# Single unread matmuls between the first products of a layer on TensorE

## The chip, the core and the metric

The kernel runs on one core of one Trainium2 chip. The core has TensorE (PE in the profile: matrix products, with PEld for the loads of its weights), VectorE (DVE), ScalarE (ACT), GpSimd (POOL) and SyncE (SP), which issues most DMAs. Each engine works through its own instructions in order and waits on semaphores for the others. The metric is the device time of one execution in microseconds, the median of several runs; lower is better.

## What is computed

An attention with two kinds of window is followed by two layers of a perceptron. All inputs and the output are float32.

```python
scores = q @ k.T / sqrt(D)            # B, H, S, D = 4, 8, 576, 64
# heads 0-3: each query sees the 32 keys up to itself
# heads 4-7: each fourth key of the 128 up to itself
attn = softmax(where(mask, scores, -1e9))
x = attn @ v                          # to 2304 tokens x 512
h = x @ w_in;  g = maximum(0.01 * h, h);                 x = g @ w_out     # 512 -> 2048 -> 512
h = x @ w_in2; g = maximum(h, 0) + log1p(exp(-abs(h)));  out = g @ w_out2
```

## The kernel before

**Stages.** Tokens are worked through in blocks. Attention runs by pairs of heads and windows of 288 tokens: transposes of q and k on PE (`pe_trans`, line 536), scores (`scores_early`, lines 585 and 589), maxima over partitions on GpSimd (line 640), the difference on VectorE (line 644), the exponential on ScalarE (line 647), the product with v (`pv`, line 665), the reciprocal and the scaling on VectorE (lines 675 to 677), a transpose back (`xT`, line 686) and a split of x into a high and a low half (lines 743 and 747).

The first layer needs a product of x with `w_in` (`g1`, "first-product", twelve matmuls of line 769) and one of the activated result with `w_out` (`g2`, "second-product", line 812), for each of 16 slices of the 2048 hidden columns. The float32 operands are split into a high and a low half, so each product takes three matmuls where one would do. The weights of the first layer come from memory as float32, are converted on ScalarE and VectorE (lines 304 to 322) and split (lines 361 and 364: the low half of a slice is the last to be ready). The second layer follows the first one.

**What sets the order.** All work is written as a list of `Op`s, each with an engine, a cost in the planner's microseconds, its dependencies and the buffers it takes and gives back. `run_schedule` goes through them in a simulated time and writes out each engine's instructions in the order that it finds. Nothing is reordered on the chip.

**Spins.** `spin(n)` (line 436) issues n matmuls that nobody reads: 288 columns of bf16 constants, into a PSUM tile in buffer y3. The list has 150 Ops of three such matmuls (`NSPIN`), each booked at 0.37 us. They are `optional`: their priority is last, and from the first first-product on (`opened`, lines 230 to 233) they are dropped without cost. Before that the planner takes one where PE has nothing ready, or, from 8 us on (`FILL`, line 208), before an operation that has just become ready. 14 such groups, 42 matmuls, are in the program.

A spin's tile is taken from a pool with one buffer for y3. A new tile in it waits until what was done with the old one is over; within one tile the three matmuls do not wait for each other. The buffer holds a bank of the attention before (a score bank, copied out by ScalarE at line 603), and of the second-product's sums from its first use on (`yp3`, line 805).

Of the kernel before, what the change touches and what calls it, by code (L numbers as in the profile page):

```python
# [26 lines left out]
def kernel(  # L27
# [80 lines left out]
    def run_schedule(slots):  # L108

        late = {"dma": 2.0, "pe": LATPE}  # L110
        lib = ["reduce"]

        def switch(o):
            return SWITCH if o.lib and o.lib != lib[0] else 0.0

        for o in ops:
            for d in o.deps:
                d.users.append(o)
            for d in o.order:
                d.next.append(o)  # L120

        def lag(a, b):
            if b.eng == "bw":
                return 2.0
            return late.get(a.eng, LATS if a.eng == b.eng else LAT) + b.slack

        left = {o: len(o.deps) + len(o.order) for o in ops}
        order = [o for o in ops if not left[o]]
        for o in order:
            for u in o.users + o.next:  # L130
                left[u] -= 1
                if not left[u]:
                    order.append(u)
        assert len(order) == len(ops)
        for o in reversed(order):
            t = [1e9 if o.target is None else o.target]
            t += [u.raw - o.cost - lag(o, u) for u in o.users]
            t += [u.raw - o.cost for u in o.next]
            o.raw = min(t)
            if o.lead is not None:  # L140
                o.earliest = max(o.earliest, o.raw - o.lead)
            o.prio = 1e6 if o.optional else o.raw - o.margin
        free = dict(slots)
        ready_at = {}
        left = {o: len(o.deps) + len(o.order) for o in ops}
        engines = sorted({o.eng for o in ops})
        pools = {e: [] for e in engines}
        busy = {e: BUSY.get(e, 0.0) for e in engines}
        events = [0.0] + list(BUSY.values())
        for o in ops:  # L150
            if not left[o]:
                ready_at[o] = o.earliest
                heapq.heappush(events, o.earliest)
                pools[o.eng].append(o)

        def done(u, t):
            left[u] -= 1
            ready_at[u] = max(ready_at.get(u, u.earliest), t)
            if not left[u]:
                pools[u.eng].append(u)  # L160
                heapq.heappush(events, ready_at[u])

        coming = {e: [] for e in engines}
        unbegun = {o: len(o.deps) + len(o.order) for o in ops}
        due = {o: o.earliest for o in ops}

        def begins(u, t):
            unbegun[u] -= 1
            due[u] = max(due[u], t)
            if not unbegun[u]:  # L170
                coming[u.eng].append(u)

        result = []
        now = locked = 0.0
        opened = False
        filled = []
        finish, held = [], []
        while True:
            moved = False
            while held and held[0][0] <= now + 1e-9:  # L180
                for r in heapq.heappop(held)[2].rel:
                    free[r] += 1
            while finish and finish[0][0] <= now + 1e-9:
                _, _, o = heapq.heappop(finish)
                if o.hold:
                    heapq.heappush(held, (o.end + o.hold, o.n, o))
                    heapq.heappush(events, o.end + o.hold)
                else:
                    for r in o.rel:
                        free[r] += 1  # L190
                for u in o.users:
                    done(u, o.end + lag(o, u))
            for e in engines:
                if busy[e] > now + 1e-9 or not pools[e]:
                    continue
                best = None
                for o in pools[e]:
                    if ready_at[o] <= now + 1e-9 and all(free[a] >= o.acq.count(a) for a in o.acq):
                        rank = o.prio + (HOLD if switch(o) else 0.0) + (WAIT if o.lock and now < locked else 0.0), o.n
                        if best is None or rank < best_rank:  # L200
                            best, best_rank = o, rank
                if best is None:
                    continue
                if e == "pe" and not opened and not best.optional and now - ready_at[best] < 0.3:

                    for o in pools[e]:
                        if o.optional and ready_at[o] <= now + 1e-9 and all(free[a] >= o.acq.count(a) for a in o.acq):
                            if result[-1:] != [o] and now > FILL and not (filled and filled[-1] is best):
                                filled.append(best)
                                best = o  # L210
                            break
                if e in ("dve", "act") and now > AHEAD_FROM:

                    soon = [u for u in coming[e] if now + 1e-9 < due[u] <= now + min(AHEAD, best.cost)
                            and u.prio < best.prio - GAP and all(free[a] >= u.acq.count(a) for a in u.acq)]
                    if soon:
                        heapq.heappush(events, min(due[u] for u in soon))
                        continue
                pools[e].remove(best)
                if best in coming[e]:  # L220
                    coming[e].remove(best)
                for a in best.acq:
                    free[a] -= 1
                best.start, best.end = now, now + best.cost + switch(best)

                if best.lib == "reduce":
                    locked = now + LOCK
                if best.lock and now < locked:
                    best.end = locked + best.cost
                if best.fn is g1:  # L230
                    opened = True
                if best.optional and opened:
                    best.end, best.skip = now, True
                if best.lib:
                    lib[0] = best.lib
                busy[e] = best.end
                heapq.heappush(finish, (best.end, best.n, best))
                heapq.heappush(events, best.end)
                for u in best.users:
                    begins(u, best.end + lag(best, u))  # L240
                for u in best.next:
                    begins(u, best.end if u.eng == e else now)
                    done(u, best.end if u.eng == e else now)
                result.append(best)
                moved = True
            if len(result) == len(ops):
                break
            if moved:
                continue
            while events and events[0] <= now + 1e-9:  # L250
                heapq.heappop(events)
            assert events, "the schedule is stuck"
            now = events[0]
        return result
# [502 lines left out]
    order = [(0, f) for f in range(LEAD)]  # L757
# [289 lines left out]
    LAG = 2  # L1047
    NCOPY = 2
    FILL = 8.0
    NSPIN, LOCK, SLACK0, SLACK, HOLDS = 150, 1.2, 0.3, 1.0, 1.5  # L1050
    SLACKT = 2.0
    AHEAD_FROM, AHEAD, GAP = 480.0, 0.9, 2.0
# [30 lines left out]
    spins = []  # L1083
    for i in range(NSPIN):
        spins.append(Op("pe", 0.37, spin, 3, order=spins[-1:], acq=["y3"], rel=["y3"], start=3.2, target=1e6, optional=True))
    y_free = {3: spins}
    reduces = []
    last_att, last_conv = [], []
    pairs, xready = [], {}
# [8 lines left out]
    for w in range(NW):  # L1098
# [3 lines left out]
        for p in range(NPAIR):  # L1102
# [14 lines left out]
            if early:  # L1117
                if p % 2 == 0:
                    ls = []
                    for which in (1, 0):  # L1120
                        qd = "dma" if which or w else "act"
                        nb = 4 if dil or w and which else 3
                        o = Op(qd, 0.48 * nb, a.load_rows, which, nc.scalar if qd == "act" else nc.sync,
                               acq=[f"rows{which}" if dil else "raw"],
                               order=[o for o in row_loads if o.earlier < w], **m)
# [5 lines left out]
            else:  # L1131
# [3 lines left out]
                           order=[] if early else [a.lq, prev(1, "lv")], **m)  # L1135
# [3 lines left out]
            if early:  # L1139
                banks = [f"y{2 * (p % 2) + which}" for which in range(2)]  # L1140
                rel = [["rows0" if dil else "raw"], ["rows1" if dil else "raw"]] if p % 2 else [[], []]
# [15 lines left out]
            if early:  # L1157
                tags = a.banks()[1]
                sc = a.o_s1 = Op("pe", 1.35 if dil else 1.15, a.scores_early, deps=[tk] + tq,
                                 order=[prev(1, "o_s1")], acq=tags + [tag_s], **ms)  # L1160
# [5 lines left out]
            else:  # L1166
                blk = 0.29 if dil else 0.33
                s0 = Op("pe", 2 * blk, a.scores, 0, deps=[tk] + tq, acq=["at", tag_s],
                        order=[prev(1, "o_s1")], **ms)
# [4 lines left out]
                   target=TR + p * 2.1 if w == 1 else None, **m)  # L1174
# [5 lines left out]
            if turned:  # L1180
                pv = a.o_pv = Op("pe", 0.9, a.pv_late, deps=x + [lv],
                                 order=[prev(1, "o_pv")], acq=["at", "xn"], **ms)
# [5 lines left out]
            for half in range(2 if dil else 1) if not turned else ():  # L1188
                pv = Op("pe", 0.58 if dil else 0.85, a.pv, half, deps=x + [lv],
                        order=pvs[-1:] or [prev(1, "o_pv")],  # L1190
# [319 lines left out]
```

## Time and profile before

| | us |
|---|---|
| three runs | 910.30, 910.72, 911.47 |
| median | 910.72 |
| profiled execution | 913.61 |
| its span, from the first to the last instruction | 911.5 |

PE is busy for 881.6 us of the span, DVE for 655.4, ACT for 393.7, POOL for 137.1. A matmul row of the profile counts as busy from its start to its modelled end, and successive matmuls overlap, so the step from one start to the next tells what a matmul costs in a stream. The granted clock of TensorE is either 2.4 GHz (1.00) or 1.2 GHz (0.50).

### The profile page before, as it was taken

The numbers are of one execution on the slowest core, as the hardware profiler recorded it, in microseconds if no ns is written. First come the engines' busy times: TensorE is split into PE (matmuls) and PEld (weight loads), VectorE is DVE, ScalarE is ACT, GpSimd is POOL, SyncE is SP. The second block draws the span as 40 slices with busy tenths as digits, with TensorE's granted clock in tenths as the row PEclk, the third lists the DMA queues.
The fourth block names the chain that finished last, engine by engine and source line by source line (L and its number), as shares of the span: only waits on it lengthen the run. The fifth ranks groups of instructions, "written<-read, shape, count | busy, mean of one in ns | idle before, by whom it ended". The sixth has DMA issues, their size and how long they took to land.

```text
span 911.5 us, 16342 instructions
## 1 busy us (share of the span) xinstructions
PE 881.6 (97%) x6376; PEld 825.5 (91%) x6376; DVE 655.4 (72%) x1189; ACT 393.7 (43%) x763; POOL 137.1 (15%) x73
## 2 busy tenths in 40 slices
PE   6889999999999999999999999999999999999998
PEld 4779999999989989998999999989888988888886
DVE  3989995476797897996975586765765775576563
ACT  2767763343344444444445563323422432243222
POOL 4500020010252351442420000000000000000000
PEclk9979999999999999999999999999999999999999
DMA  8879122255545455454237877632453353235332
GB/s 228 224 212 307 21 36 50 75 121 169 164 112 157 113 148 172 131 145 165 88 117 262 278 251 222 194 93 93 139 156 101 115 172 105 93 116 144 111 93 93
DMA packets 157985, 131.89 MB, mean 145 GB/s; under 512 B 102100, under 2 KB 138964, under 8 KB 157908
## 3 DMA queue, kind: packets, MB, share of 16 engines
q1 hardware_dynamic: 155508, 130.26, 48.3%
q8 instruction: 50, 0.82, 0.4%
q10 hardware_dynamic: 2400, 0.59, 0.3%
q14 instruction: 27, 0.22, 0.1%
HBM read 104.60 MB, written 26.21 MB: 144 GB/s over the span
## 4 chain that ended last, share of the span: by engine, by line
PE 51%; DVE 2%; POOL 0%; issue 0%; ACT 0%; POOLq 0%
PE yo L1018 22%; PE h L945 17%; PE yp L812 5%; PE h L769 4%; PE hp L1006 2%; DVE cf L322 0%; DVE cf L313 0%; POOL mx L640 0%; PE sc L616 0%; DVE xn L712 0%; DVE gl L794 0%; DVE cs L332 0%; PE pv L696 0%; DVE rd L717 0%; DVE s L644 0%
## 5 line engine op out<-in xcount | busy, mean ns | idle before, releaser
L812 PE MATMUL yp<-gh,w 128*128 128x288 f32 (+2 forms) x1024 | 230.1, 299 | 4.1 <-DVE ys L822 2.0
L769 PE MATMUL h<-xh,w 128*128 128x288 f32 (+2 forms) x1024 | 231.2, 301 | 1.1 <-DVE w L364 1.1
L1018 PE MATMUL yo<-wo,w 128*128 128x512 f32 x864 | 222.9, 395 | 0.0
L945 PEld LDWEIGHTS h<-tr,w 128*128 128x128 f32 x1344 | 174.4, 188 | 11.1
L812 PEld LDWEIGHTS yp<-gh,w 128*128 128x128 f32 x1024 | 171.8, 188 | 6.3 <-DVE ys L822 3.5
L1018 PEld LDWEIGHTS yo<-wo,w 128*128 128x128 f32 x864 | 152.5, 188 | 27.1
L945 PE MATMUL h<-tr,w 128*128 128x256 f32 x1344 | 176.8, 279 | 0.0
L769 PEld LDWEIGHTS h<-xh,w 128*128 128x128 f32 x1024 | 173.0, 190 | 2.4 <-DVE w L364 1.6
L769 PE MATMUL h<-xl,w 128*128 128x288 f32 (+2 forms) x512 | 152.2, 297 | 0.7 <-DVE xl L747 0.7
L812 PE MATMUL yp<-gl,w 128*128 128x288 f32 (+2 forms) x512 | 151.0, 295 | 0.3 <-DVE gl L794 0.3
L983 ACT ACTIVATE ex<-ex 128x512 f32<-128x512 f32 x72 | 45.5, 632 | 152.2 <-DVE ex L980 151.9
L785 ACT ACTIVATE hc<-h 128x288 f32<-128x288 f32 (+2 forms) x128 | 51.8, 404 | 109.9 <-PE h L769 108.7
L769 PEld LDWEIGHTS h<-xl,w 128*128 128x128 f32 x512 | 97.2, 190 | 1.2 <-DVE xl L747 1.2
L812 PEld LDWEIGHTS yp<-gl,w 128*128 128x128 f32 x512 | 96.2, 188 | 0.6 <-DVE gl L794 0.5
L794 DVE TENSOR_TENSOR gl<-hc,gh 128x288 fp32r<-128x288 f32 (+2 forms) x128 | 65.3, 512 | 36.1 <-ACT gh L790 35.4
L640 POOL PARTITION_ALL_REDUCE mx<-s x24 | 50.0, 2084 | 268.3 <-DVE s L630 244.2
L986 DVE SCALAR_TENSOR_TENSOR ex<-hs,ex 128x512 f32<-128x512 f32 x64 | 44.3, 692 | 32.8 <-ACT ex L983 32.3
L704 POOL PARTITION_ALL_REDUCE sm<-s x16 | 61.6, 3850 | 39.2 <-ACT s L647 39.2
L304 ACT ACTIVATE cf<-raw 128x512 f32<-128x512 f32 (+1 forms) x48 | 39.9, 831 | 57.0 <-DMA raw<-in_moe_w_in_dram 30.0
L991 ACT ACTIVATE w<-ex 128x512 fp32r<-128x512 f32 x72 | 45.3, 629 | 34.1 <-DVE ex L986 34.1
L995 DVE TENSOR_TENSOR w<-ex,w 128x512 fp32r<-128x512 f32 x72 | 49.7, 691 | 11.7 <-ACT w L991 6.8
L790 ACT ACTIVATE gh<-hc 128x288 fp32r<-128x288 f32 (+2 forms) x128 | 56.7, 443 | 3.0
(103 smaller groups left out, 980.8 us busy)
## 6 DMA issues: line engine op xcount, KB each, us to landing
wo<-w2o SPq DMA_DIRECT2D x80, 512.0 KB
raw<-in_moe_w_in_dram SPq DMA_DIRECT2D x32, 512.0 KB
raw<-in_moe_w_out_dram SPq DMA_DIRECT2D x32, 512.0 KB
w2o<-cf SPq DMA_DIRECT2D x16, 512.0 KB
out_dram<-o SPq DMA_DIRECT2D x36, 128.0 KB
w2a<-cf SPq DMA_DIRECT2D x8, 512.0 KB
w2s<-cs SPq DMA_DIRECT2D x8, 512.0 KB
w<-w2a SPq DMA_DIRECT2D x8, 512.0 KB
```

The source lines that it names most:

```text
L640: nc.gpsimd.partition_all_reduce(self.mx, self.sf, channels=P, reduce_op=bass_isa.ReduceOp.max)
L704: nc.gpsimd.partition_all_reduce(self.sm, self.sf, channels=P, reduce_op=bass_isa.ReduceOp.add)
L769: nc.tensor.matmul(out=h, lhsT=a[:, c, :], rhs=b_[:, c, :], start=(c == 0 and a is whi and b_ is xh), stop=(c == NC - 1 and a is wlo))
L785: nc.scalar.activation(out=hc, in_=hbank.pop(s), func=AF.Prelu, alpha=0.01)
L790: nc.scalar.activation(out=gh, in_=hcopy[s], func=AF.Copy)
L794: eng.tensor_sub(out=gl, in0=hcopy.pop(s), in1=gparts[s][0].bitcast(F32))
L812: nc.tensor.matmul(out=ybank[e][:, o:o + n], lhsT=a[:, e * P:(e + 1) * P], rhs=b_, start=(f == 0 and n == unit_len[u] and a is whi and b_ ...
L945: nc.tensor.matmul(out=bank[m, b][:, half], lhsT=w[:, a, kb * P:(kb + 1) * P], rhs=t[:, b_, kb], start=(kb == 0 and a + b_ == 0), stop=(kb ...
L983: nc.scalar.activation(out=self.ex, in_=self.ex, func=AF.Softplus)
L991: nc.scalar.activation(out=self.gh, in_=self.ex, func=AF.Copy)
L995: nc.vector.tensor_sub(out=self.gl, in0=self.ex, in1=self.gh.bitcast(F32))
L1018: nc.tensor.matmul(out=obank[c, t], lhsT=a, rhs=b_, start=(opens and n == 0), stop=(closes and n == 2))
```

## The change

51 single spins are put into PE's instructions between the first first-product and the first second-product. A second list of 160 optional Ops, `fills`, stands behind the old list: `spin(1)`, one matmul and one tile each, booked at 0.125 us. They are dropped only from the first second-product on (`closed`), and are passed over while an operation of PE becomes due within the next 0.2 us of the planner's time. The groups of three are dropped from the first first-product on as before.

```diff
-        opened = False
+        opened = begun = closed = False
...
+                        if o.optional and o.args[0] == 1 and begun and not closed and any(
+                                u is not o and not u.optional and now < due[u] < now + 0.2 for u in coming["pe"]):
+                            continue
...
-                if best.fn is g1:
-                    opened = True
-                if best.optional and opened:
+                begun = begun or best.fn is g1
+                closed = closed or best.fn is g2
+                opened = begun
+                if best.optional and (closed if best.args[0] == 1 else begun):
                     best.end, best.skip = now, True
...
+    NFILL = 160
...
-    y_free = {3: spins}
+    fills = []
+    for i in range(NFILL):
+        fills.append(Op("pe", 0.125, spin, 1, order=(fills or spins)[-1:], acq=["y3"], rel=["y3"], target=1e6, optional=True))
+    y_free = {3: spins + fills}
```

The instructions of VectorE, ScalarE, GpSimd and SyncE stand in the order of before. On PE the 51 spins, each with a load of its weights, stand in five trains: 5 behind the first first-product, 17 behind the transposes that follow it, 14 behind the next P·V (sixteen matmuls in the profile, eight here), 3 behind the second first-product, 12 behind the next transposes. The old instructions of PE keep their order among themselves. The line numbers of the changed kernel are higher by 4 in the functions shown here (spin 443, transpose 690, P·V 669, first-product 773).

PE before, from the end of the first first-product (`h_644`) over the transposes (`xt`) and P·V (`pv`) to the second first-product (`h_717`); what stands in brackets is the engines or DMA queues that the instruction waits for:

```order
L769 MATMUL h_644<-xh_489,w_496 128x256
L686 MATMUL xt_678<-ident_85,xn_625 128x96 [waits DVE_49,PE_49]
L686 MATMUL xt_678<-ident_85,xn_625 128x96 x2
L665 MATMUL pv_697<-lent_102 72x65 [waits DMAHW5_49,PE_49,Activation_49]
L665 MATMUL pv_697<-lent_102 72x65 [waits DMAHW6_49]
L665 MATMUL pv_697<-lent_102 72x65 x2
L665 MATMUL pv_703<-lent_102 72x65 [waits DVE_49,PE_49]
L665 MATMUL pv_703<-lent_102 72x65 x3
L769 MATMUL h_717<-xh_489,w_672 128x256
```

PE in the changed kernel, around the same transposes (now `xt_688`), with the last spins of the first train and the first of the second:

```order
L443 MATMUL spin_682<-masksb_88,identb_87 128x288 [waits PE_49]
L443 LDWEIGHTS identb_87
L443 MATMUL spin_684<-masksb_88,identb_87 128x288 [waits PE_49]
L690 MATMUL xt_688<-ident_85,xn_625 128x96 [waits DVE_49]
L690 MATMUL xt_688<-ident_85,xn_625 128x96 x2
L443 LDWEIGHTS identb_87
L443 MATMUL spin_699<-masksb_88,identb_87 128x288 [waits PE_49]
L443 LDWEIGHTS identb_87
L443 MATMUL spin_701<-masksb_88,identb_87 128x288 [waits PE_49]
```

Each spin is a tile of its own (another number) with a wait for PE; the first of all waits for ScalarE instead.

PE in the changed kernel, from the end of the second train over the same P·V (now `pv_741`, `pv_747`) to the third train:

```order
L443 MATMUL spin_736<-masksb_88,identb_87 128x288 [waits PE_49]
L669 MATMUL pv_741<-lent_102 72x65 [waits DMAHW5_49,Activation_49]
L669 MATMUL pv_741<-lent_102 72x65 [waits DMAHW6_49]
L669 MATMUL pv_741<-lent_102 72x65 x2
L669 MATMUL pv_747<-lent_102 72x65 [waits DVE_49]
L669 MATMUL pv_747<-lent_102 72x65 x3
L443 LDWEIGHTS identb_87
L443 MATMUL spin_752<-masksb_88,identb_87 128x288 [waits PE_49]
```

P·V stands behind 17 spins and ahead of 14 where it stood between the transposes and the second first-product.

## Rows read from the trace of the kernel before

**Rows 1.** The page's first part: busy us, share of the span, instructions.
```profile
PE 881.6 (97%) x6376; PEld 825.5 (91%) x6376; DVE 655.4 (72%) x1189; ACT 393.7 (43%) x763; POOL 137.1 (15%) x73
```

**Rows 2.** Table by stage: length, busy us (instructions) by engine, granted clock, DMA share, GB/s.
```profile
0.00:15.80 15.80, 6.97 (x28) 4.03 (x29) 6.03 (x4) 1.54 (x2) 7.39 (x23) 1.00 0.92 257
15.80:44.80 29.00, 25.76 (x300) 21.46 (x298) 22.97 (x39) 22.46 (x49) 15.59 (x9) 1.00 0.79 210
44.80:49.90 5.10, 3.35 (x36) 3.06 (x34) 5.03 (x12) 3.32 (x9) 2.47 (x1) 1.00 0.40 76
49.90:60.15 10.25, 8.15 (x46) 7.63 (x45) 7.86 (x18) 7.90 (x12) 0.00 (x0) 0.50 0.69 176
60.15:911.50 851.35, 837.35 (x5977) 789.37 (x5975) 613.47 (x1119) 358.53 (x693) 111.62 (x40) 1.00 0.47 140
...
60.00:130.00 70.00, 70.00 (x601) 69.81 (x600) 67.66 (x100) 52.26 (x83) 6.69 (x3) 1.00 0.50 154
```

**Rows 3.** PE in order of time: start us, us, instruction, [idle before, releaser].
```profile
46.16 0.28 PE L769 MATMUL h<-xh,w 128*128 128x256 f32 x1
46.27 0.41 PE L686 MATMUL xt<-ident,xn 96*128 96x96 f32 x3
48.29 1.58 PE L665 MATMUL pv<-lent 104*72 104x65 f32 x16 [1.60 <-ACT lent L647]
49.67 0.36 PE L769 MATMUL h<-xh,w 128*128 128x256 f32 x1
...
51.34 0.80 PE L769 MATMUL h<-xh,w 128*128 128x256 f32 x2 [1.09 <-DVE w L364]
...
53.64 0.68 PE L686 MATMUL xt<-ident,xn 72*128 72x72 f32 x4
55.34 1.23 PE L665 MATMUL pv<-lent 104*72 104x65 f32 x8 [1.01 <-ACT lent L647]
56.32 0.56 PE L769 MATMUL h<-xh,w 128*128 128x256 f32 x1
...
59.03 1.15 PE L665 MATMUL pv<-lent 104*72 104x65 f32 x8
59.97 0.47 PE L808 MATMUL yp<-zero,identb 128*128 128x512 bf16 x1
...
62.63 0.28 PE L769 MATMUL h<-xh,w 128*128 128x256 f32 x1
...
64.03 0.28 PE L812 MATMUL yp<-gh,w 128*128 128x256 f32 x1
```

**Rows 4.** Spins by stretch: duration ns min/median/max, first and last start us.
```profile
L439 PE MATMUL spin<-masksb,identb x21: 397/444/448, 8.5 to 14.5; 128*128 128x288 bf16 x21
...
L439 PE MATMUL spin<-masksb,identb x21: 283/284/296, 16.5 to 41.9; 128*128 128x288 bf16 x21
```

**Rows 5.** PE in order of time, in small windows at two groups of spins.
```profile
8.91 0.45 PE L439 MATMUL spin<-masksb,identb 128*128 128x288 bf16 x1
9.42 0.40 PE L439 MATMUL spin<-masksb,identb 128*128 128x288 bf16 x1
...
41.41 0.42 PE L686 MATMUL xt<-ident,xn 72*128 72x72 f32 x4
41.66 0.53 PE L439 MATMUL spin<-masksb,identb 128*128 128x288 bf16 x3
41.91 0.28 PE L439 MATMUL spin<-masksb,identb 128*128 128x288 bf16 x1
42.03 0.28 PE L585 MATMUL sc<-masksb,identb 128*128 128x288 bf16 x1
42.25 0.28 PE L585 MATMUL sc<-masksb,identb 128*128 128x288 bf16 x1
```

**Rows 6.** Who waited for whom, 44.7 to 64 us, DVE: us in total, times, longest.
```profile
DVE rd L675 <- PE pv L665: 2.1, 2, 1.7
```

**Rows 7.** The same for PE from 60 us to the end.
```profile
PE sc L616 <- DVE xn L724: 2.3, 2, 1.6
...
PE yp L812 <- DVE gl L794: 0.3, 1, 0.3
```

## The prediction, made before the run

> **What bounds the kernel now.** I read the busy table of the page first: TensorE (PE) is busy 97% of the span, VectorE (DVE) 72%, the others less [rows 1]. Then the table by stage, for where the missing 3% lies and at which clock PE works [rows 2]. From 60.15 us to the end PE is busy 837.35 of 851.35 us at granted clock 1.00, and from 60 to 130 us without any gap. So past 60 us the end is set by PE, and what shifts the first second-product (line 812, at 59.97) shifts nearly everything behind it. Ahead of that lies the stretch that the change touches: 44.8 to 49.9 with PE busy 3.35 of 5.10 us at clock 1.00, and 49.9 to 60.15 with PE busy 8.15 of 10.25 us at clock 0.50, that is 1.2 instead of 2.4 GHz.
>
> Third comes the order of PE's work in that stretch [rows 3]. Three idle times are to be seen: 1.60 us ahead of the product P·V at 48.29 (for the exponential on ScalarE), 1.09 ahead of the third matmul of the second first-product at 51.34 (for the low half of its weights on DVE), and 1.01 ahead of P·V at 55.34 (exponential again). And the same work costs more at the lower level: the twelve matmuls of a first-product take 2.71 us (56.32 to 59.03) and 1.40 us at the full one (62.63 to 64.03); eight matmuls of P·V take 0.94 us (59.03 to 59.97) against half of 1.38 (sixteen, 48.29 to 49.67), 0.69. So of what could be had here, the 3.70 us of idle time are not in a fill's reach, since other engines end them; the slow clock is.
>
> **What the change adds.** By the order of instructions nothing moves on DVE, ScalarE, GpSimd or the DMA queues. PE gets 51 matmuls of 288 columns ("spins", line 439), each with a weight load: 5 after the first first-product, 17 after the transpose behind it, 14 after the P·V that follows, 3 after the second first-product, 12 after the transposes behind that. The planner books 0.125 us for each. That is the pace of spins that don't wait for each other: three take from 41.66 to 42.03, 0.12 us each [rows 5].
>
> But these don't run so. A spin of the old kind is one tile of three matmuls; a new one is a tile of its own in the same PSUM buffer y3, and so each carries a wait for PE itself: it starts when the one before it has ended (all but the first of the 51 have that wait). What such a wait costs can be read off twice in the trace of before [rows 5]. At the full clock: the third spin of a group starts at 41.91 and takes 0.28; the second score matmul (line 585), which goes into the same buffer and waits for that spin, starts at 42.25. That is 0.34 us from start to start instead of 0.12. At the lower level, where spins take 444 ns at the median and not 284 [rows 4]: a group's last spin starts at 8.91 and takes 0.45, and the next group, which waits for it, starts at 9.42, so 0.06 us after its end. A spin that starts a group takes 0.40 there, so a single one costs 0.40 + 0.06 = 0.46 us, and at most 0.51 (8.91 to 9.42). The last spin of a train costs only its streaming, 0.12 or 0.24 us, where what follows doesn't wait for it.
>
> **The sum with the clock full throughout.** A train of n spins takes (n-1) x 0.34 + 0.12: 1.48, 5.56, 4.54, 0.80 and 3.86 us. PE's path, from the end of the first first-product at 46.27 [rows 3]: train of 5 to 47.75; transposes 0.25 (as 41.41 to 41.66, [rows 5]) to 48.00; train of 17 to 53.56; sixteen P·V 1.38 to 54.94; train of 14 to 59.48; first-product 1.40 to 60.88; train of 3 to 61.68; transposes 0.25 to 61.93; train of 12 to 65.79; P·V 0.69 to 66.48; first-product 1.40 to 67.88; P·V 0.69 to 68.57. Before, the second-product was reached at 59.97: 8.6 us later. The three idle times of before are inside this (what ended them, at 48.29, 51.34 and 55.34, is long there), and so is the gain from the clock. Nothing else is late: the engines that fed PE here run as before until they come to something that PE delays, DVE at the reciprocal of P·V (line 675), which already stood for PE twice, 2.1 us in all [rows 6]. DVE takes its work in order, so it stands there and doesn't run ahead. The delay thus passes to it whole.
>
> **The clock.** Whether the spins hold it is the open cost. In before it fell at 49.9, in a stretch with PE partly idle, and came back at 60.15, after PE had worked without a gap from 55.34 [rows 2, 3]. A self-waiting spin streams for 0.12 of its 0.34 us. And the trace shows a stretch of spins with self-waits that did not bring the clock up: 21 of them from 8.5 to 14.5 us, the fastest 397 ns, all at the lower level, with one wait in three spins rather than in each [rows 4]. (The stage table writes 1.00 for 0 to 15.8; the durations say otherwise.) So I take it that trains of 17, 14 and 12 such spins don't hold the full clock, and that it falls at about 49.9 as before. How long it stays down has two ends: not at all, 8.6 us in sum; or until the second-product. For the latter: of the train of 17, six steps at 0.34 and ten at 0.46, to 48.00 + 2.04 + 4.60 + 0.24 = 54.88; P·V 1.88 to 56.76; train of 14, 13 x 0.46 + 0.24 = 6.22, to 62.98; first-product 2.71 to 65.69, which is 4.8 us behind the sum above; then train of 3 +0.4, transposes +0.25, train of 12 +1.4, P·V +0.25, first-product +1.3, P·V +0.25, in all 3.9 more: 8.6 + 4.8 + 3.9 = 17.3 us. Between them I take the clock low from 49.9 to the end of that first-product, the first work without waits that PE meets, and full behind it: 8.6 + 4.8 = 13.4 us. This is nearest to the row of before, where gapless work brought it back.
>
> A rule bears on this. The Trainium skill (TensorE: Matmul & The Clock Gate, "Why this matters for your kernels") puts drops of the clock in mid-kernel down to longer idle gaps between bursts of matmuls. By it these spins, 0.06 us apart, hold the clock, and the sum is the 8.6 us of the first rival. The trace doesn't quite agree: here the clock fell with no gap of PE longer than 1.60 us.
>
> **From the profile to the time.** The profiled execution took 913.61 us with a span of 911.5, 2.1 us outside it, and lies 2.9 us over the median of the three runs, 910.72. With 13.4 us more it would be 927.0 with a span of 924.9. On the median: 910.72 + 13.4 = 924.1 us.
>
> **Rivals.**
> - *The spins hold the clock.* For it: a spin is in flight for 0.28 of each 0.34 us, and PE never stands idle for longer than 0.06. Against it: the 21 spins at the start. Time: 910.72 + 8.6 = 919.3 us.
> - *The self-waits cost nothing, and the fills do what the planner booked.* Then the trains take 0.61, 2.07, 1.71, 0.37 and 1.46 us, and the same path gives: transposes at 46.88, P·V at 49.20, first-product at 52.29, transposes at 54.06, P·V at 55.77, first-product at 56.46, second-product at 57.86 + 0.69 = 58.55, 1.4 us earlier than before: 909.3 us, faster than before. For it: the work at the lower level is there to be won, and the weights and exponentials are ready by then. Against it: 41.91 to 42.25. There are 46 steps from spin to spin, so it turns into a loss from a step of 0.12 + 1.4/46 = 0.15 us on; the row shows 0.34.
> - *The delay is given back behind 60 us.* PE waits there six times over for DVE and ScalarE, from 2.3 us for scores to 0.3 for a low half [rows 7], 9.4 us in all six rows. If those engines were ahead by then, that could be saved: 924.1 - 9.4 = 914.7 us. Against it: they stand in order behind work that PE delays, above all DVE at line 675, and DVE is busy 67.66 of the 70 us from 60 to 130 [rows 2], so it can't get ahead.
>
> **How the numbers follow.** Clock lost for part of the stretch (924.1): 0.55. Clock held (919.3): 0.32. Fills without cost (909.3): 0.07. Given back (914.7): 0.06. A measurement of this kernel can tell about 0.2% (1.8 us) from no change. The third case, at -0.15%, lies inside this bound by its sum and outside it with a little more, so I split it: faster 0.03, same 0.04, slower 0.93. The range leaves out the last two cases, 0.13. Its low end is the held clock less some tenths, 918.5; its high end the clock low to the second-product, 910.72 + 17.3 = 928.0, with half of what steps of 0.51 in place of 0.46 would add (36 such steps, 1.8 us): 929.
>
> **What would show it.** In the profile after, spins at 46.3 to about 70 us that start 0.34 us apart at the full clock and about 0.46 at the lower one; no idle time ahead of P·V and the first-products, since PE comes there last; DVE idle for several us ahead of line 675; the first second-product at 68 to 77 us instead of 59.97; from there on the same picture as before, shifted. If the clock reads 1.00 through the stretch, the first rival holds; if the spins start 0.12 us apart, the second; if the second-product is late by more than the end of the span, the third. The forecast is wrong altogether if a spin's wait for its predecessor is free.

## The result and the profile after

The changed kernel takes 920.92 us (median of four runs, 919.92 to 922.90) against 910.53 for the kernel before: 1.0115 of its time, 95% interval 1.0096 to 1.0133, 10.4 us more. The forecast was 924.1 us in a range of 918.5 to 929.0. This kernel's time moves by some us from execution to execution and between chips (on the three chips of the experiments the kernel before had medians of 913.16, 912.92 and 910.90, with single runs from 909.3 to 920.4), so the experiments are compared by their ratio to the kernel before on the same chip, and by stages of their traces.

The table by stage of the changed kernel (length, busy us and instructions of PE, PEld, DVE, ACT, POOL, granted clock, DMA share, GB/s) answers to [rows 2]. 45.45 is the end of the first first-product (46.27 before), 71.55 about the start of the first second-product (59.97 before):

```profile
45.45:51.26 5.81, 4.92 (x23) 1.92 (x22) 5.10 (x7) 3.63 (x8) 1.25 (x1) 1.00 0.51 92
51.26:64.90 13.64, 12.58 (x50) 6.85 (x50) 4.25 (x10) 2.35 (x5) 0.00 (x0) 0.50 0.85 248
64.90:71.55 6.65, 6.04 (x45) 3.91 (x45) 2.21 (x6) 3.33 (x7) 0.00 (x0) 1.00 1.02 372
71.55:917.80 846.25, 836.57 (x5978) 789.45 (x5977) 614.89 (x1120) 359.82 (x695) 111.81 (x40) 1.00 0.45 136
```

The clock still falls, 51.26 instead of 49.9, and is down longer: 13.64 us instead of 10.25. PE's order of time in the stretch answers to [rows 3]:

```profile
45.33 0.27 PE L773 MATMUL h<-xh,w 128*128 128x256 f32 x1
45.45 1.65 PE L443 MATMUL spin<-masksb,identb 128*128 128x288 bf16 x5
46.94 0.41 PE L690 MATMUL xt<-ident,xn 96*128 96x96 f32 x3
47.18 6.27 PE L443 MATMUL spin<-masksb,identb 128*128 128x288 bf16 x17
53.25 2.11 PE L669 MATMUL pv<-lent 104*72 104x65 f32 x16
55.16 6.34 PE L443 MATMUL spin<-masksb,identb 128*128 128x288 bf16 x14
61.12 0.59 PE L773 MATMUL h<-xh,w 128*128 128x256 f32 x1
...
63.86 1.28 PE L443 MATMUL spin<-masksb,identb 128*128 128x288 bf16 x3
64.97 0.42 PE L690 MATMUL xt<-ident,xn 72*128 72x72 f32 x4
65.23 4.01 PE L443 MATMUL spin<-masksb,identb 128*128 128x288 bf16 x12
69.08 0.68 PE L669 MATMUL pv<-lent 104*72 104x65 f32 x8
69.57 0.37 PE L773 MATMUL h<-xh,w 128*128 128x256 f32 x1
...
71.06 0.68 PE L669 MATMUL pv<-lent 104*72 104x65 f32 x8
71.60 0.47 PE L816 MATMUL yp<-gh,w 128*128 128x256 f32 x1
```

No row carries an idle time any more, where three did: PE has become the last to come everywhere. It counts as busy on the profile's page, 893.4 us against 881.6, but much of a spin's row is its wait: 5 of them take 1.49 us from 45.45 to 46.94, 4 x 0.34 + 0.12. VectorE and ScalarE wait now (44.7 to 75 us; before, VectorE 2.1 us for P·V [rows 6] and 0.2 for `xh`, ScalarE 2.4 for `h`):

```profile
DVE rd L679 <- PE pv L669: 7.1, 2, 3.8
DVE xl L751 <- ACT xh L747: 7.0, 1, 7.0
ACT hc L789 <- PE h L773: 14.6, 2, 11.3
```

VectorE's 7.0 us for `xh` (58.9 to 65.9) come by way of ScalarE, which stood 11.3 us (52.8 to 64.1) for the second first-product and splits x only behind it.

### The profile page after: what moved, and what is told of

It is laid out like the page before. It is cut to its first block, busy times and chain, and to the rows that moved or that the text cites. A ratio compares the mean times of both kernels' runs of the same rounds, so it can differ in the third digit from the quotient of the medians.

```text
span 917.8 us, 16439 instructions
## 1 busy us (share of the span) xinstructions
PE 893.4 (97%) x6426; PEld 828.4 (90%) x6427; DVE 656.9 (72%) x1189; ACT 394.4 (43%) x763; POOL 137.3 (15%) x73
## 4 chain that ended last, share of the span: by engine, by line
PE 50%; DVE 2%; POOL 0%; issue 0%; ACT 0%; POOLq 0%
PE yo L1022 22%; PE h L949 17%; PE yp L816 4%; PE h L773 4%; PE hp L1010 2%; DVE cf L326 0%; DVE cf L317 0%; POOL mx L644 0%; DVE gl L798 0%; DVE xn L716 0%; DVE cs L336 0%; PE sc L620 0%; DVE s L648 0%; PE pv L700 0%; DVE qz L575 0%
## 5 line engine op out<-in xcount | busy, mean ns | idle before, releaser
L949 PEld LDWEIGHTS h<-tr,w 128*128 128x128 f32 x1344 | 174.3, 188 | 11.1
L1022 PEld LDWEIGHTS yo<-wo,w 128*128 128x128 f32 x864 | 152.5, 188 | 27.1
L999 DVE TENSOR_TENSOR w<-ex,w 128x512 fp32r<-128x512 f32 x72 | 49.8, 691 | 11.7 <-ACT w L995 6.8
```

What stands on the lines that cost most here:

```text
L949: nc.tensor.matmul(out=bank[m, b][:, half], lhsT=w[:, a, kb * P:(kb + 1) * P], rhs=t[:, b_, kb], start=(kb == 0 and a + b_ == 0), stop=(kb ...
L999: nc.vector.tensor_sub(out=self.gl, in0=self.ex, in1=self.gh.bitcast(F32))
L1022: nc.tensor.matmul(out=obank[c, t], lhsT=a, rhs=b_, start=(opens and n == 0), stop=(closes and n == 2))
```

## Experiments

### The kernel before, and the changed one, a second time

The kernels are unchanged: e1 is the kernel before, e5 the changed one.

> The kernel before once more, for a second trace. The forecast was 13.4 us more; on PE's path up to the first second-product the two traces differ by 12.4 us (13.70 from the end of the first first-product before, 26.1 after), but the spans differ by only 6.3 us and the medians by 10.4. Theory 1: the first trace of before was a long execution (2.9 us over the median), with more waiting of PE behind 60 us (9.4 us in all) than is usual; then this one has about 6 to 7 us of such waits and a span near 908.6. Theory 2: the waits behind 60 us are always 9 to 10 us in this kernel, and the changed kernel gives some 4 us of its delay back there; then they are 9 to 10 us again here and the span is 908 to 909 for another reason.

> The changed kernel once more, beside e8 on one chip. Its first trace had the second-product 12.4 us later by PE's path and a span only 6.3 us (against the first trace of before) or 9.4 us (against the second, e1) longer. Theory 1 (what came back behind 60 us was chance: VectorE stood for a DMA of the second layer's weights for 1.0 us there, 4.5 to 8.2 in three of the other traces): this time the waits of PE behind 60 us are 7 to 9 us again, and the time is 920 to 924. Theory 2 (a late second-product always gets some 4 us back): 5 us of waits again, 919 to 921.

e1 took 910.5 us in its single run, 2.7 us under the median of the kernel before on its chip, with a span of 908.4. PE's waits behind 60 us add up to 8.6 us (9.4 in the first trace), which lies between the two theories of e1 and nearer to theory 2. Whether the changed kernel gives something back there is left to e5. In e1 the clock was down for a shorter time than in the first trace, 6.82 us:

```profile
45.40:51.20 5.80, 2.87 (x29) 2.37 (x28) 5.73 (x11) 3.72 (x8) 1.26 (x1) 1.00 0.47 85
51.20:58.02 6.82, 5.71 (x35) 5.50 (x33) 5.68 (x13) 5.27 (x10) 0.00 (x0) 0.50 0.84 222
```

e5 took 924.03 us (922.11 to 926.50), 1.0127 of the kernel before, interval 1.0105 to 1.0150. Its second-product starts at 73.72, 27.8 us behind the end of the first first-product at 45.88, since the clock fell twice, from 52.40 to 66.05 and again from 69.47 to 72.88. PE's waits behind 60 us are 8.4 us, where the first trace of the changed kernel had 5.3, and nothing of the delay is given back in its span, 923.7:

```profile
52.40:66.05 13.65, 12.69 (x53) 7.38 (x53) 4.24 (x10) 2.33 (x5) 0.00 (x0) 0.50 0.90 278
69.47:72.88 3.41, 3.35 (x20) 3.17 (x19) 1.79 (x4) 0.00 (x0) 0.00 (x0) 0.50 0.53 194
```

So theory 1 of e5 is borne out, its time at the very top of what theory 1 gave: what came back behind 60 us in the first trace does not come back whenever the second-product is late. From the second-product to the end of the span it is 851.5 us in the first trace of before, 850.0 in e1, 850.0 in e5, and 850.3 and 851.5 in e3 and e8 below, which are also late. The first trace of the changed kernel has 846.2, the least of all; the other traces, none of them so late, have 847.7 to 852.6. Why that one execution was shorter stays open. VectorE's wait for the store of a converted weight piece (line 313, `w2s`, 75 to 480 us) was 1.0 us in it, 4.9 in the first trace of before and 3.4 in e5, but PE's waits don't follow it: e3 has 8.2 us of it and 7.2 us of waits of PE.

### All spins in one tile: without the wait

```diff
+    filler = {}
+
+    def fill(n):
+        if "ps" not in filler:
+            filler["ps"] = ps_y.tile([P, NI * QP], F32, tag="y3", name="spin")
+        for i in range(n):
+            nc.tensor.matmul(
+                out=filler["ps"], lhsT=ident_b, rhs=masks_b.rearrange("p i m -> p (i m)"), start=True, stop=True)
...
-                o.fn(*o.args)
+                if o.fn is spin and o.args[0] == 1:
+                    fill(1)
+                else:
+                    o.fn(*o.args)
```

> The changed kernel with all 51 single spins in one tile, so that none waits for the one before it; number and places are the same. Theory (the wait for the predecessor is the cost): spins start 0.12 us apart, the trains take 0.61, 2.07, 1.71, 0.37 and 1.46 us, the clock stays at 1.00, the second-product is reached 1.4 us earlier than in the kernel before, and the time is 909.1 us (908.3 to 910.3). Rival (it is the 51 matmuls as such, or where they stand): 915 us or more.

Measured 909.0 us (906.43 to 910.32), 0.9941 of the kernel before, interval 0.9921 to 0.9961. The same 51 matmuls at the same places, and only the first one waits. PE in order of time, and then the stage table:

```profile
46.17 0.79 PE L452 MATMUL spin<-masksb,identb 128*128 128x288 bf16 x5
46.79 0.41 PE L699 MATMUL xt<-ident,xn 96*128 96x96 f32 x3
47.04 2.25 PE L452 MATMUL spin<-masksb,identb 128*128 128x288 bf16 x17
49.13 1.20 PE L678 MATMUL pv<-lent 104*72 104x65 f32 x16
```

```profile
45.00:58.00 13.00, 13.00 (x127) 11.76 (x126) 12.48 (x27) 10.60 (x20) 2.43 (x1) 1.00 0.64 154
```

17 spins now take 2.09 us (47.04 to 49.13) instead of 6.07, the clock stays at 1.00 from 45 to 58 us, and the second-product starts near 57.9, 11.7 us behind the first first-product: 2.0 us less than in the first trace of before, 1.2 less than in e1 (45.4 to about 58.3, 12.9), and 14.4 less than in the changed kernel. So the wait is the cost, and spins at the pace that the planner books are a gain of 0.4 to 0.8%.

### Two buffers in turn: half the wait

```diff
...
+            tag = ("y3", "y2")[filler[0] % 2]
+            filler[0] += 1
+            ps = ps_y.tile([P, NI * QP], F32, tag=tag, name="spin")
...
```

> The 51 single spins as in the changed kernel, each a tile of its own, but in two PSUM buffers in turn (y3 and y2), so that each waits for the last but one. Theory (the wait sets the step): the step is half of 0.34, 0.17 us, the trains take 0.80, 2.84, 2.33, 0.46 and 1.99 us, the clock holds or falls for a short time, and PE's path from the first first-product to the second-product is 14.5 us (13.7 before, 26.1 in the changed kernel): 911.3 us (910 to 914). Rival (each tile of its own costs its 0.34 us whatever it waits for): 920.9.

Measured 911.3 us (908.73 to 917.93), 0.9988 of the kernel before, interval 0.9967 to 1.0009. This is as expected, and not told apart from the kernel before. PE in order of time, and then the stage table:

```profile
45.24 0.98 PE L453 MATMUL spin<-masksb,identb 128*128 128x288 bf16 x5
46.06 0.41 PE L700 MATMUL xt<-ident,xn 96*128 96x96 f32 x3
46.31 3.00 PE L453 MATMUL spin<-masksb,identb 128*128 128x288 bf16 x17
49.15 1.20 PE L679 MATMUL pv<-lent 104*72 104x65 f32 x16
```

```profile
45.20:59.00 13.80, 13.80 (x116) 10.25 (x116) 11.31 (x23) 9.36 (x17) 1.30 (x1) 1.00 0.62 147
```

17 spins take 2.84 us (46.31 to 49.15), 16 x 0.17 + 0.12, to the hundredth what half the step gives. The stretch is 13.8 us long with the clock kept, as long as with the idle times and the slow clock in the first trace of before (13.7). The rival is out: each spin still has a tile of its own, but with twice the distance to the last one in its buffer the step is half as long.

### Trains as long, without waits: the clock's part

```diff
+        trains, inside = [12, 46, 37, 7, 32], False
         for o in schedule:
...
+            if o.fn is spin and o.args[0] == 1:
+                if not inside:
+                    fill(trains.pop(0))
+                    inside = True
+                continue
...
```

Here `fill` is that of e2, so all spins are in one tile.

> As e2, but with trains of 12, 46, 37, 7 and 32 spins in one tile: each train is as long as the changed kernel's would be at the full clock (1.48, 5.56, 4.54, 0.80, 3.86 us), without self-waits. Theory (the self-waiting spins lost the clock, and that cost 3 to 4 us on top of their length): clock 1.00 throughout, second-product 8.6 us later than in the kernel before, time some 3 to 4 us under the changed kernel's, 917 to 919. Rival (the length of the trains is all, the clock costs nothing): the changed kernel's 920.9. Second rival (part of any delay is given back behind 60 us): 914 to 916.

> e3 once more, beside e5 on one chip, to price the clock: both have trains of the same length at the full clock, but only the changed kernel's wait for themselves. Theory (the clock lost 4.2 us on PE's path, 26.1 against 21.9): 3 to 4 us faster than e5. Rival (the length of the trains is all): the same as e5.

e3 took 919.84 us (918.33 to 920.60), 1.0064 (1.0042 to 1.0086), a little over the 917 to 919 expected; e8 921.21 (919.24 to 926.53), 1.0104 (1.0077 to 1.0131). The times alone, 0.6 and 1.0% over the kernel before, would leave room for the rival in which some of the delay is given back; the traces don't, with 850.3 and 851.5 us from the second-product to the end. The stage from the end of the first first-product to the second-product, e3 and then e8:

```profile
45.50:67.50 22.00, 22.00 (x200) 18.72 (x200) 11.60 (x23) 9.47 (x17) 1.31 (x1) 1.00 0.78 233
```

```profile
45.20:67.10 21.90, 21.90 (x200) 18.66 (x199) 11.49 (x23) 9.36 (x17) 1.24 (x1) 1.00 0.78 214
```

Both keep the clock at 1.00 through 134 spins without waits, and take 21.9 us over the stretch. That is 8.2 us more than before, near the 8.6 that the sum gives for the clock held, and 4.2 us less than the changed kernel's 26.1, or 5.9 less than the 27.8 of e5. In the traces, then, the clock costs the changed kernel 4 to 6 us. By the times it is less clear: e8 is 2.8 us faster than e5 on the same chip (3 to 4 expected), but the intervals of the two ratios overlap. The rival without a cost of the clock is out by the stage tables; by the times alone it is not.

### Trains that fit the idle times

The loop is that of e3, first with the trains of e4 and e9, all in one tile:

```diff
...
+        trains, inside = [0, 12, 9, 0, 8], False
...
```

and then with those of e7 and e10, where `fill` calls `spin(1)`, so that each has its wait:

```diff
+    def fill(n):
+        for i in range(n):
+            spin(1)
...
+        trains, inside = [0, 5, 4, 0, 3], False
...
```

> As e2, but with trains of 0, 12, 9, 0 and 8 spins, so that each about fills the idle time of the kernel before and doesn't outlast it. Theory: P-V starts at 48.3 as before, the second first-product at 51.1 and ends a microsecond earlier at the full clock, the exponential behind it comes earlier, and the second-product is reached 2.5 to 3 us earlier: 907.8 us (907 to 909). Rival (the clock falls with these few spins too, or the gain is given back to VectorE behind 60 us): 910.5, no change.

> As e4, idle times filled and not outlasted, but with self-waiting single spins at 0.34 us a step: trains of 0, 5, 4, 0 and 3 instead of 0, 12, 9, 0 and 8. Theory (self-waiting spins don't hold the clock): it falls at about 50 us as in the kernel before, nothing is won, 910.5 us. Rival (any spin in flight holds it; the changed kernel only had too many): the time of e4, 907.4, with clock 1.00.

e4 took 907.4 us (906.22 to 909.09), 0.9928 (0.9903 to 0.9953); e7 910.41 (908.02 to 917.15), 0.9985 (0.9965 to 1.0005). e4 gained more against its chip's 913.16 than was expected (0.7% for 0.3%). By the times the theory of e7 seemed right, by the trace it wasn't. The stretch to the second-product, e4 and then e7:

```profile
45.20:56.40 11.20, 10.09 (x95) 8.51 (x94) 10.99 (x23) 9.10 (x17) 1.30 (x1) 1.00 0.60 154
```

```profile
46.10:57.30 11.20, 9.48 (x78) 6.85 (x78) 10.99 (x23) 9.09 (x17) 1.31 (x1) 1.00 0.68 167
```

Both take 11.2 us at clock 1.00: with twelve self-waiting spins in short trains the clock stayed up as with 29 dense ones. In e7's trace the clock had fallen earlier, at 32 us, ahead of all fills, and come back at 39. So both ran once more on one chip.

> e4 once more, beside e10 on one chip. In their traces PE's path from the first first-product to the second-product is the same, 11.1 us (e4: 45.25 to about 56.3; e7: 46.16 to 57.27), against 13.7 in the kernel before, and the clock is 1.00 through it in both; yet e4 took 907.4 us on one chip and e7 910.4 on another. Theory 1 (the difference is the chip, or clock falls ahead of the stretch, as at 32 us in e7's trace, which have nothing to do with the self-wait): the same time as e10, both 2 to 3 us under the kernel before. Theory 2 (self-waiting spins lose the clock in most executions, only not in the one that was traced): e10 is 2 to 3 us slower than this one.

> e7 once more, beside e9 on one chip: theory 1 the same time as e9, 907 to 908.5; theory 2 2 to 3 us more than e9, about the kernel before.

e9 took 906.73 us (906.27 to 907.73), 0.9961 (0.9946 to 0.9976); e10 908.77 (906.93 to 913.38), 0.9980 (0.9967 to 0.9993). Neither theory holds as it stood. e10 is 2.0 us behind e9, as theory 2 has it, but the two intervals overlap, and its trace shows again a fall ahead of the fills, as theory 1 has it, which held until they began:

```profile
33.13:53.61 20.48, 20.21 (x131) 18.35 (x131) 14.60 (x33) 11.70 (x23) 5.89 (x3) 0.50 0.77 203
53.61:63.50 9.89, 8.49 (x74) 6.33 (x73) 9.27 (x21) 8.60 (x16) 0.00 (x0) 1.00 0.79 226
```

From 53.61 on, with the self-waiting spins, the clock is 1.00. Of e10's twelve runs the three with a mean granted clock of 0.999 or 1.000 took 906.9 to 908.5 us, the others, at 0.988 to 0.997, 907.4 to 913.4. Whether those lost the clock before the fills, as the traced one, or within them, the runs don't tell, since there is one trace of each label. e4 and e9 are the fastest kernels here, 0.4 to 0.7% under the kernel before.

## Why the prediction was right, point by point

**The wait is the cost: right.** The step that decided, that a single spin waits for the one before it and so costs 0.34 us and not the 0.125 of the planner, holds to the hundredth: 1.49 us for five against 1.48 forecast, 3.85 for twelve against 3.86. e2 shows it by taking the wait away, e6 by halving it. The rival in which waits cost nothing is what e2 shows once the wait is gone: its second-product comes 1.2 to 2.0 us earlier than before, where the rival had 1.4. That the times are alike too, 909.0 and 909.3, is in part luck: e2 is 0.6% under the kernel before on its chip, the rival's sum 0.2%.

**The clock: right that it falls, and a little too dear.** Where the time of the stretch went, with the fall at 49.9 and the return at the end of the second first-product as forecast, and as measured:

| | forecast us | measured us |
|---|---|---|
| train of 5 and transposes | 1.48 + 0.25 | 1.49 + 0.24 |
| train of 17 | 6.88 | 6.07 |
| P·V, sixteen | 1.88 | 1.91 |
| train of 14 | 6.22 | 5.96 |
| first-product | 2.71 | 2.74 |
| train of 3 and transposes | 0.80 + 0.25 | 1.11 + 0.26 |
| train of 12 | 3.86 | 3.85 |
| P·V, first-product, P·V | 0.69 + 1.40 + 0.69 | 0.49 + 1.49 + 0.54 |
| in all | 27.1 | 26.1 |

The clock returned at 64.9, one train of 3 after the first-product that was to bring it back. It fell 4.1 us into the train of 17 and not 1.9, which is most of the 0.8 us on that train; a step at the lower level was 0.44 (train of 14: 13 steps in 5.96 - 0.24) and not 0.46. e5, with 27.8 us and two falls, lies on the other side of the forecast, so the size was a fair middle of two executions, and in part luck. The forecast let gapless work bring the clock back; in e10 PE is busy 20.21 of 20.48 us at 0.50 and the clock stays down, and the falls of the traces last from 3.4 us (e3) to those 20.5. The rival in which the clock holds is out for this kernel by the 0.50 in both of its traces, and e3 shows what it would have been.

**The reason given for the clock: not borne out.** The forecast said that trains of 17, 14 and 12 self-waiting spins would not hold it, from 21 spins at the start of the kernel, in groups that wait for each other, that did not bring it up. The fall came true in the train of 17, and in e5 once more at the end of the train of 12. But the 21 spins were those of one trace. In nine of the twelve traces (not in before, e5 and e10) the durations drop from 444 to 283 ns within the same 21 spins, as here in e7, in the last of them:

```profile
L443 PE MATMUL spin<-masksb,identb x10: 282/283/320, 11.7 to 13.5; 128*128 128x288 bf16 x10
```

And e7 shows short trains of single spins, between P·V and first-products, at 1.00. So it isn't the self-wait as such that keeps the clock down. What is shown is narrower: in both traces of the changed kernel the clock fell within a long self-waiting train, and in none of the six with spins 0.17 us apart or closer (e2, e3, e4, e6, e8, e9) did it fall in the stretch. In both traces of the kernel before it fell at about the same place, 49.9 and 51.2, without any such spin, so what made it fall at 51.26 stays open.

The rule that was weighed, from the Trainium skill (TensorE: Matmul & The Clock Gate, "Why this matters for your kernels"), that drops come of longer idle gaps, doesn't agree with this trace: the fall at 51.26 follows spins whose starts were 0.34 us apart, without an idle time in any row of the stretch.

**What follows behind: right in the main.** Nearly all of the delay went to VectorE (14.1 us of waiting in two rows, 2.3 before), but only half of it, 7.1 us, at the line that the forecast named; the other 7.0 came by way of ScalarE, which stood for the second first-product. The delay came out at the end: against e1, whose stretch is 12.9 us, the first trace of the changed kernel is 13.2 us longer in the stretch and 9.4 in the span, e5 14.9 in the stretch and 15.3 in the span. The rival in which 9.4 us come back is out; once, 3.8 did, and in e5, e3 and e8 next to none.

**The total.** 13.4 us were forecast; 10.4 were measured first and 11.1 by e5's median against the kernel before on its chip. In the first trace two terms are behind the difference: the stretch is 1.0 us shorter than forecast, and part of the delay did not reach the end of the span, by chance if e5 is any guide. In e5's trace the stretch is 14.1 us longer than in the first trace of before, more than was forecast; but this execution took 925.84 us, 1.8 over e5's median, and the 11.1 us are counted from 912.92, 2.2 over the 910.72 that the forecast started from. The traces thus show the terms of the sum, and the total only to some us.

## What to carry to other kernels

A filler instruction should not wait for its predecessor: put fillers that nobody reads into one tile, since a new tile in the same buffer brings a wait for the old one's completion, and that turned 0.12 us into 0.34 for these matmuls. When a planner books a cost, look in the trace for a row in which the instruction stands with just the waits that it will have. And let a fill end before the work that it bridges to: with 51 dense spins (e2) the stretch takes 11.7 us, with 29 (e4, e9) 11.2, by one trace each; the ratios of e2 and e4 (0.9941 and 0.9928) do not tell them apart.

## What the runs showed of the hardware

The granted clock falls at other places from one execution of a program to the next, and much of this kernel's spread goes with it. On one chip the kernel before took 910.1 us in a run with a mean granted clock of 0.996 and 920.4 us in one with 0.981; over its 18, 23 and 17 runs on three chips the time and the mean granted clock are correlated by -0.91, -0.76 and -0.91. The kernels are alike up to 45 us, and the clock fell at 32 or 33 us in the traces of e2, e7 and e10 and not in the other nine. It fell for 3.4 us further on too, in e3 and e8 right behind PE's wait of 1.88 us for VectorE ahead of scores at 272.8 and 272.4, in e6 behind one of 2.06 us at 292.6, in e7 behind waits of 1.26 and 0.51 us at 416.4 and 417.5. The falls at 32 us come beside a wait of PE of 1.4 us for ScalarE, which is there in every trace (1.2 in e1), with PE busy 3.4 to 3.6 us from 29 to 34 us (3.41 in e4, clock 1.00; 3.41 in e10, 0.91). So the same work was granted either level. The rise at the start moves too: the first spin is at 8.5 us, and the spins take 283 ns from about 12 us on in e7, but still 397 or more at 14.5 in the first trace of before.
